# Two tiles of the first product at a time, by seven products of quarters in place of eight

## The chip, the cores and the metric

The kernel runs on one core of a Trainium2 chip. The metric is the device time of one execution in microseconds (us), shown as the median of several runs. Engines are named as in the profile: PE (TensorE) multiplies matrices, DVE (VectorE), ACT (ScalarE) and POOL (GpSimd) do everything else on the data, SP (SyncE) issues the transfers (DMA). Each engine works through its instructions in the order in which they were written; a wait stops everything behind it on that engine, SP's queue of transfers included. [...]

## The reference

Windowed attention (8 batches, 8 heads, 576 tokens, 64 channels a head), and on its output a feed-forward block for 4608 tokens:

```
x = attention(q, k, v)                     # 4608 x 512; half the heads see 32 neighbours, half every 4th of 128
h = x @ w_in                               # first product, 512 -> 1024
e = exp(h - max(h)); sm = e / (sum(e) + 1e-9)
solu = h * sm
ln = (solu - mean) / sqrt(var + 1e-6) * g_ln
out = ln @ w_out                           # second product, 1024 -> 512
```

## The kernel before

The 4608 tokens are 36 tiles of 128; attention is done in 32 units (a batch's pair of heads each). Matmuls run on fp32r operands. Since one such number doesn't hold all of an fp32, every operand is split into a high and a low part, and each product is three matmuls: high by high, high by low, low by high. So the first product of a tile (`moe_h`, L335 to L347) is 4 (parts of the 512 inputs) x 2 (halves of the 1024 outputs) x 3 = 24 matmuls of 128x128 by 128x512, and the second (`moe_o`, L473) is 24 as well.

The work is written out by hand as lists of words. `OPENING` (L50) holds the loading and splitting of the weights, the first units and tiles. Then the loop over tiles i = 6 to 35 (L582) runs the list `STEP` (L77) once a step: a word's name is the operation, its suffix says on which tile or unit (i the present tile, j and k the one and two before; n and m units of attention that run ahead). What a step does, in words:

- `ha hb hc hd`: first product of tile i on PE into banks 2 and 3 (L141; the same two banks for every tile from 3 on).
- `peak e gate mid var`: maximum on DVE (L352), exp on ACT (L359), h times exp with its sum on DVE (L366), minus the mean on DVE (L382), square on ACT (L387), then six tiny instructions on POOL that end in `rstd` (L388 to L395). `gate` is the last to read h from the banks.
- `forth back`: the tile goes to DRAM and comes back in another order (L439, L446, on SP's queue); `trA trB` turn it in 32x32 blocks on DVE (L455), `thA thB` make the high part on ACT (L463), `tlA tlB` the low part on POOL (L468). `o` is the second product on PE (L477), `out` scales on ACT (L487) and stores.
- `S mask max sub exp sum inv norm turn V`: one unit's attention: scores on PE (L211), mask, maximum, sums and the turn on DVE, `sub` on POOL (L250), exp on ACT (L254), and `V` on PE (L289).
- `xh xl`: high part of attention's output on ACT (L314), low part on DVE (L328), into the rings `x_hi` and `x_lo`, which hold two batches.
- `q v`: loads of a later unit (L165, L173), four buffers each.

The last tile is turned by PE (`t`, L412) instead of by way of DRAM.

## Time and profile before

| | us |
|---|---|
| median of 3 runs | 516.84 (516.23 to 517.65) |
| the profiled execution | 515.99 |
| its span, first to last instruction | 514.2 |
| PE busy, share of the span | 482.4, 94% |
| DVE, ACT, POOL busy | 343.0, 235.2, 218.5 |
| a first or second product without attention between, 24 matmuls | 5.44 |

The span is less than the execution's time by what lies around it, 1.8 us. Busy shares are means over stages with different limits. In the profile's rows, "out<-in" names tiles, L the line of the kernel; a group's row gives its count, busy time in us, the mean of one in ns, and the idle time ahead of it with what ended that.

### The profile page before, as it was taken

The page shows a single profiled execution, that of the slowest core. Times are in us where ns is not written, and L with a number is a line of the kernel's source. Part 1 is how long each engine was busy: PE and PEld are TensorE (multiplying, and loading weights), DVE is VectorE, ACT ScalarE, POOL GpSimd, SP SyncE. Part 2 cuts the span into 40 slices and gives each one's busy share as a digit, 9 for nine tenths or more (in the row PEclk, how much of TensorE's full clock was granted, in tenths as well). Part 3 has the DMA queues.
Part 4 walks back from the last instruction along what each step waited for, and adds up shares of the span by engine and source line. Part 5 has one row for each costly group of instructions (what it writes and reads, how often), then busy time and mean ns, then how long its engine had stood idle before and what let it go on. Part 6 is the DMA issues. An engine that isn't in the chain of part 4 may idle for free.

```text
span 514.2 us, 16377 instructions
## 1 busy us (share of the span) xinstructions
PE 482.4 (94%) x7132; PEld 388.2 (75%) x7132; DVE 343.0 (67%) x539; ACT 235.2 (46%) x387; POOL 218.5 (42%) x342
## 2 busy tenths in 40 slices
PE   1359989999999999999999999999999999999997
PEld 1237767788788888888888888888877888888885
DVE  3999999766467765577677766576677776444540
ACT  3857888633344443344433344343434444333351
POOL 1634775634444443444434443444444334333360
PEclk9999999999999999999999999999999999999999
DMA  7969186636585664556655564646644333333331
GB/s 274 402 234 376 46 286 197 197 125 212 169 273 184 184 180 137 153 183 182 182 169 172 181 182 137 183 154 184 177 141 134 105 106 91 111 108 103 108 98 61
DMA packets 47304, 88.37 MB, mean 172 GB/s; under 512 B 5504, under 2 KB 23808, under 8 KB 47232
## 3 DMA queue, kind: packets, MB, share of 16 engines
q1 hardware_dynamic: 47232, 87.32, 53.2%
q8 instruction: 56, 0.92, 0.7%
q14 instruction: 16, 0.13, 0.1%
HBM read 59.51 MB, written 27.79 MB: 170 GB/s over the span
## 4 chain that ended last, share of the span: by engine, by line
PE 90%; DMA 4%; DVE 3%; SPq 1%; issue 0%; ACT 0%; ACTq 0%; DVEq 0%
PE banks L341 40%; PE banks L477 39%; PE banks L289 6%; PE banks L211 5%; DMA raw<-w_in 1%; DMA kt<-kT 1%; DMA qt<-qT 1%; DVE low L526 1%; DVE pt L273 0%; DVE mag L534 0%; DVE rs L258 0%; PE banks L203 0%; DVE sm L247 0%; DVE mx L237 0%; SPq L165 0%
## 5 line engine op out<-in xcount | busy, mean ns | idle before, releaser
L341 PE MATMUL banks<-w_i,x_hi 128*128 128x512 f32 x576 | 183.1, 399 | 0.5 <-DVE mu L366 0.4
L477 PE MATMUL banks<-w_o,th 128*128 128x512 f32 x576 | 181.0, 395 | 0.0
L341 PEld LDWEIGHTS banks<-w_i,x_hi 128*128 128x128 f32 x576 | 106.6, 190 | 24.6 <-DVE mu L366 1.0
L477 PEld LDWEIGHTS banks<-w_o,th 128*128 128x128 f32 x576 | 106.2, 188 | 22.1 <-DVE w_o L548 0.2
L341 PE MATMUL banks<-w_i,x_lo 128*128 128x512 f32 x288 | 113.0, 393 | 0.0
L477 PE MATMUL banks<-w_o,tl 128*128 128x512 f32 x288 | 112.2, 390 | 0.0
L468 POOL TENSOR_TENSOR tl<-t,th 128x512 fp32r<-128x512 f32 x70 | 89.7, 1299 | 41.1 <-ACT th L463 41.1
L352 DVE TENSOR_REDUCE nmax<-banks 128x1 f32<-128x1024 f32 x36 | 44.0, 1223 | 65.2 <-PE banks L341 65.2
L254 ACT ACTIVATE sm<-sm 128x640 f32<-128x640 f32 x32 | 23.5, 736 | 94.5 <-POOL sm L250 94.0
L359 ACT ACTIVATE e<-banks,nmax 128x1024 f32<-128x1024 f32 x36 | 40.2, 1117 | 51.4 <-DVE nmax L352 50.8
L341 PEld LDWEIGHTS banks<-w_i,x_lo 128*128 128x128 f32 x288 | 54.5, 189 | 11.7
L477 PEld LDWEIGHTS banks<-w_o,tl 128*128 128x128 f32 x288 | 54.1, 188 | 11.7
L387 ACT ACTIVATE e<-t 128x1024 f32<-128x1024 f32 x35 | 37.2, 1062 | 55.2 <-DVE t L382 55.2
L366 DVE CUSTOM_DVE_ANT_0 t<-banks,e 128x1024 f32<-128x1024 f32 x36 | 43.9, 1219 | 17.1 <-ACT e L359 17.0
L289 PEld LDWEIGHTS banks<-pt,vt 32*64 32x64 f32 x2816 | 34.8, 138 | 18.9 <-issue 11.3
L463 ACT CAST th<-t 128x512 fp32r<-128x512 f32 x70 | 41.7, 619 | 15.9 <-DVE t L455 8.6
L455 DVE STREAM_TRANSPOSE t<-raw 128x512 f32<-128x512 f32 x70 | 44.9, 677 | 3.8 <-issue 2.6
L225 DVE TENSOR_TENSOR sm<-banks,mask_sb 128x640 f32<-128x640 f32 x22 | 18.1, 824 | 44.0 <-PE banks L211 43.8
L250 POOL TENSOR_TENSOR sm<-sm,mx 128x640 f32<-128x640 f32 x27 | 34.5, 1276 | 29.7 <-DVE mx L237 26.7
L289 PE MATMUL banks<-pt,vt 32*64 32x64 f32 (+3 forms) x2816 | 38.1, 234 | 7.7 <-DVE pt L273 7.7
L392 POOL TENSOR_SCALAR sq<-sq 128x1 f32<-128x1 f32 x36 | 7.7, 215 | 86.1 <-ACT e L387 85.6
L388 POOL TENSOR_SCALAR se<-se 128x1 f32<-128x1 f32 x36 | 8.7, 243 | 77.3 <-ACT e L359 76.6
(62 smaller groups left out, 474.7 us busy)
## 6 DMA issues: line engine op xcount, KB each, us to landing
mid<-t SPq DMA_DIRECT2D x140, 128.0 KB, 2.3
raw<-mid SPq DMA_DIRECT2D x35, 512.0 KB, 3.5
vt<-vw SPq DMA_DIRECT2D x32, 384.0 KB, 4.0
kt<-kT SPq DMA_DIRECT2D x32, 312.0 KB, 4.2
qt<-qT SPq DMA_DIRECT2D x32, 296.0 KB, 4.6
out<-ob SPq DMA_DIRECT2D x36, 256.0 KB, 2.1
t<-w_in SPq DMA_DIRECT2D x5, 512.0 KB, 7.2
t<-w_out SPq DMA_DIRECT2D x4, 512.0 KB, 6.7
```

The lines of the kernel that those rows point to most:

```text
L211: nc.tensor.matmul(out=ps[WIN * c : WIN * c + WIN, h, WQ * i : WQ * i + WQ], lhsT=qt[D * h : D * h + D, q0 : q0 + WIN], rhs=kt[D * h : D * ...
L250: eng.tensor_tensor(out=st[n]["sm"], in0=st[n]["sm"], in1=wide(mx), op=ALU.subtract)
L289: nc.tensor.matmul(out=ps_x[D * h : D * h + D, c, c0 : c0 + k1 - k0], lhsT=vt[WIN * c : WIN * c + WIN, i, D * h : D * h + D], rhs=pt[WIN * ...
L341: nc.tensor.matmul(out=ps_h(i)[:, half], lhsT=a[:, kt, xs], rhs=w_i[:, kt, half, part, :], start=(kt == 0 and k == 0), stop=(kt == KT - 1 ...
L352: nc.vector.tensor_reduce(out=nmax, in_=h, axis=AX.X, op=ALU.max, negate=True)
L359: nc.scalar.activation(out=e, in_=h, func=AF.Exp, bias=nmax, scale=1.0, accum_out=se)
L366: nc.vector.tensor_tensor_reduce(out=t, in0=h, in1=ms[i]["e"], scale=1.0, scalar=0.0, op0=ALU.mult, op1=ALU.add, accum_out=mu,)
L387: nc.scalar.activation(out=e, in_=t, func=AF.Square, accum_out=sq)
L455: nc.vector.transpose(out=turned(i)[:, cut(c)].rearrange("p k (a r) -> p k a r", r=WIN), in_=ms[i]["mv"].rearrange("p (a k s) -> p k a s", ...
L463: nc.scalar.copy(out=ms[i]["th"][:, cut(c)], in_=turned(i)[:, cut(c)])
L468: nc.gpsimd.tensor_tensor(out=ms[i]["tl"][:, cut(c)], in0=turned(i)[:, cut(c)], in1=ms[i]["th"][:, cut(c)].bitcast(F32), op=ALU.subtract,)
L477: nc.tensor.matmul(out=ps_o(i), lhsT=a[:, f, :], rhs=w_o[:, f, part, :], start=(f == 0 and k == 0), stop=(f == FT - 1 and k == 2),)
```

## The change

Tiles 0 to 13 are done as before. Tiles 14 to 35 go in eleven pairs (pair r is tiles 2r and 2r + 1, r from 7 to 17). For a pair, x is cut into four quarters (tile a or b, first or second half of the 512 inputs) and `w_in` into four. Seven products of sums of quarters, P1 to P7, give the four quarters of h that took eight before. A product of quarters is 6 matmuls, so 42 a pair in place of 48. It needs:

- sums of quarters of `w_in` (`fa` to `fh`), made once, on POOL, then their high parts on ACT (`Th`) and low parts on DVE (`Tl`). They are written behind the words of steps 8 to 12 (`BEHIND`). They take the room of two of four buffers of q, k and v, so units from 12 on have two.
- sums of quarters of x for each pair (`z1` to `z4`, on POOL, from fp32 values), split into high (`hS12 hS34`, ACT) and low (`lS12 lS34`, POOL); the plain quarters are split too (`hA1 hA2` on ACT, `lA1 lA2` on DVE). For that, x of units 16 and later stays in fp32 and is copied into the rings by a transfer (`xd`) from where ACT put it (`xf`). The sums for pair 7 stand ahead of step 13's words, their splits behind.
- sums of products: P1, P6, P7 and P4 follow one another in bank 0, P2 is in bank 1, P5 and P3 are in bank 2. ACT copies three stages out (`s1`, `s2`, `s5`), and DVE adds a bank to such a copy and takes the maximum in one instruction (`c11 c12 c22 c21`). So h stands in SBUF, and `e` and `gate` read it there.

The pairs have a list of their own, `PAIR`, and the last pair `LAST_PAIR`; the last tile goes by way of DRAM as the others do. Attention runs up to four units ahead throughout, and ends with unit 31 in pair 14; before, it ended with tile 30.

The diff, cut to its core (`a` and `b` are the pair's tiles, `c` and `d` those of the pair before, s the next pair; u, w, x and y units):

```diff
+AHEAD = {13: "z1.s z2.s z3.s z4.s "}
+BEHIND = {
+    8: "fa0 fb0 fc0 fd0", 9: "fe0 ff0 fg0 fh0 Th0 Th4 Th2 Th6", 10: "Tl0 Tl4 Tl2 Tl6 fa1 fb1 fc1",
+    11: "fd1 fe1 ff1 fg1 fh1 Th1 Th5 Th3 Th7", 12: "Tl1 Tl5 Tl3 Tl7",
+    13: "back.i hS12.s lS12.s hS34.s lS34.s",
+}
+PAIR = (
+    "P1.r trB.c P5.r S.u mask.u P2.r s1.r trA.c s5.r max.u c11.r q.u P6.r thB.c tlB.c V.x thA.c "
+    "trA.d tlA.c s2.r sub.u xf.x xd.x v.x exp.u P7.r P3.r trB.d z1.s sum.u S.w c12.r inv.u "
+    "thA.d pk.a thB.d oA.c tlA.d e.a mask.w tlB.d c22.r z2.s hS12.s gate.a oB.c mid.a max.w "
+    "forth.a P4.r norm.u z4.s z3.s c21.r hA1.s out.c sub.w var.a oA.d oB.d exp.w turn.u pk.b "
+    "V.y hA2.s e.b lA1.s sum.w hS34.s back.a inv.w lS12.s out.d gate.b mid.b norm.w lS34.s "
+    "forth.b q.w var.b back.b turn.w xf.y xd.y lA2.s v.y "
+)
+LAST_PAIR = (
+    "trA.c P1.r P2.r trB.c thA.c s1.r P6.r thB.c tlA.c tlB.c c11.r trA.d P5.r s2.r thA.d trB.d "
+    "P7.r s5.r thB.d tlA.d tlB.d P3.r c22.r P4.r c12.r pk.a c21.r e.a oA.c oB.c pk.b gate.a "
...
+POOL_WORDS = "z1 z2 z3 z4 lS12 lS34".split()
...
+    def t_value(j, kt, half):
+        add(nc.gpsimd, value(j), f32(w_i[:, kt, half, 0]), f32(w_i[:, kt, half, 1]))
+    def t_minus(j, a, b):
+        subtract(nc.gpsimd, value(j), value(a), value(b))
+    def t_hi(n):
+        nc.scalar.copy(out=t_high(n), in_=value(n // 2 + 1))
+    def t_lo(n):
+        subtract(nc.vector, t_low(n), value(n // 2 + 1), f32(t_high(n)))
...
+            if j == 1:
+                add(eng, out, x_of(b, 0, 2, c), x_of(b, 2, 4, c))
+            elif j == 2:
+                subtract(eng, out, v[1][:, :, c], x_of(a, 0, 2, c))
+            elif j == 3:
+                subtract(eng, out, x_of(a, 0, 2, c), x_of(b, 0, 2, c))
+            else:
+                subtract(eng, out, x_of(a, 2, 4, c), v[2][:, :, c])
...
+        bank = {1: 0, 6: 0, 7: 0, 4: 0, 2: 1, 5: 2, 3: 2}[j]
+        for kt in range(2):
+            for k, (pa, pb) in enumerate(((0, 0), (0, 1), (1, 0))):
+                nc.tensor.matmul(
+                    out=banks[:, bank],
+                    lhsT=left(pa, kt),
+                    rhs=right(pb, kt),
+                    start=j in (1, 2, 5) and kt == 0 and k == 0,
+                    stop=kt == 1 and k == 2,
...
+    def snap(i, half, bank):
+        nc.scalar.copy(out=part_h(i, half), in_=banks[:, bank])
+    def finish(i, half, bank, key):
+        mx = ms[i][key] = small.tile([P, 1], F32, name=key)
...
+        nc.vector.tensor_tensor_reduce(
+            out=out, in0=banks[:, bank], in1=zero.broadcast_to([P, 512]) if plain else out,
+            scale=1.0, scalar=LOWEST, op0=ALU.add, op1=ALU.max, accum_out=mx,
+        )
```

Where the change puts POOL's additions. Before, POOL's row between steps 9 and 10: the end of one step's `var`, then the low part `tl` of the tile whose second product comes next, then `sub`, then `var` again.

```order
L392 TENSOR_SCALAR sq_2504<-sq_2504 128x1
L393 TENSOR_TENSOR s2_2507<-s2_2507,sq_2504 128x1
L395 TENSOR_TENSOR rstd_2512<-s2_2507,mhalf_84 128x1
L468 TENSOR_TENSOR tl0_2551<-t0_2297,th0_2547 128x512 x2
L250 TENSOR_TENSOR sm0_2610<-sm0_2610,mx_2612 128x640
```

The same place on POOL now (`kt3`, `vt3` and `x` are buffers that hold the sums of quarters):

```order
L434 TENSOR_SCALAR sq_2501<-sq_2501 128x1
L435 TENSOR_TENSOR s2_2504<-s2_2504,sq_2501 128x1
L437 TENSOR_TENSOR rstd_2509<-s2_2504,mhalf_84 128x1
L512 TENSOR_TENSOR kt3_2339<-vt3_2344,kt3_2339 128x512
L512 TENSOR_TENSOR vt3_2344<-vt3_2344,qt3_2341 128x512
L515 TENSOR_TENSOR x_2543<-w_i_86 128x512
L512 TENSOR_TENSOR x_2543<-x_2543,vt3_2344 128x512
L482 TENSOR_TENSOR tl0_2561<-t0_2287,th0_2557 128x512 x2
L278 TENSOR_TENSOR sm0_2620<-sm0_2620,mx_2622 128x640
```

Four additions have come between `var` and `tl`. On ACT at the same place now stand four splits of these sums (L558) ahead of `th` (L477) and of the unit's exp (L282); the last, from `x`, needs the last of the four additions.

```order
L502 ACTIVATE ob_2538<-banks_90,rstd_2148 128x512
L558 CAST tp_2546<-qt3_2341 128x512
L558 CAST qt2_2548<-kt3_2339 128x512
L558 CAST more_2550<-vt3_2344 128x512
L558 CAST vt2_2552<-x_2543 128x512
L477 CAST th0_2557<-t0_2287 128x512 x2
L282 ACTIVATE sm0_2620<-sm0_2620 128x640
```

On ACT in the last pair, the copies of banks (L700: `s1`, `s2` into `t2`, `s5` into `t3`) stand between the high parts of the two tiles before (`th0` of tile 32, `th1` of tile 33):

```order
L477 CAST th0_6798<-t0_6614 128x512
L700 COPY t2_6800<-banks_90 128x512
L477 CAST th0_6798<-t0_6614 128x512
L700 COPY t2_6800<-banks_90 128x512
L477 CAST th1_6822<-t1_6617 128x512
L700 COPY t3_6831<-banks_90 128x512
L477 CAST th1_6822<-t1_6617 128x512
```

The third copy is behind the first half of tile 33's high part; before, the only word of the last tile at such a place was its exp.

## The prediction

> **What bounds the kernel now.** I read the page first: its span and its line of busy shares.

> ```profile
> span 514.2 us, 16377 instructions
> PE 482.4 (94%) x7132; PEld 388.2 (75%) x7132; DVE 343.0 (67%) x539; ACT 235.2 (46%) x387; POOL 218.5 (42%) x342
> ```

> PE alone is near the span. So I read the chain of waits in order of time over one step of the loop, that of tile 10 (below, 0 of a step is the first matmul of its first product):

> ```profile
> 169.44 2.72 PE banks L341 x12
> 172.16 0.97 PE banks L211 x64
> 173.13 2.95 PE banks L341 x12
> 176.08 1.13 PE banks L289 x76
> 177.21 5.71 PE banks L477 x24
> 182.91 1.13 PE banks L341 x5
> ```

> The chain never leaves PE: first product in two halves with the scores between them, attention, second product; 182.91 - 169.44 = 13.47 us a step, and 2.72 / 12 = 0.227 us a matmul. Fewer matmuls pay as long as the other engines keep up. How much room they have I read from their timeline in the same step:

> ```profile
> 171.12 2.53 POOL L468 TENSOR_TENSOR tl<-t,th 128x512 fp32r<-128x512 f32 x2 [1.14 <-ACT th L463]
> 174.93 1.26 POOL L250 TENSOR_TENSOR sm<-sm,mx 128x640 f32<-128x640 f32 x1 [1.28 <-DVE mx L237]
> 176.22 0.74 ACT L254 ACTIVATE sm<-sm 128x640 f32<-128x640 f32 x1 [4.58 <-POOL sm L250]
> 177.43 1.12 ACT L359 ACTIVATE e<-banks,nmax 128x1024 f32<-128x1024 f32 x1 [0.48 <-DVE nmax L352]
> 178.45 0.19 ACT L359 ACTIVATION_READ_ACCUMULATOR e<-banks,nmax 128x1 f32 x1
> 179.93 0.08 DVE L366 DVE_READ_ACCUMULATOR2_ANT mu<- 128x1 f32 x1
> 180.24 0.75 DVE L382 TENSOR_SCALAR t<-t,mu 128x1024 f32<-128x1024 f32 x1
> 182.05 0.18 ACT L387 ACTIVATION_READ_ACCUMULATOR e<-t 128x1 f32 x1
> 182.42 0.85 DVE L273 STREAM_TRANSPOSE pt<-sm 128x640 f32<-128x640 f32 x1
> 182.88 0.57 POOL L395 TENSOR_TENSOR rstd<-s,mhalf 128x1 f32<-128x1 f32 x1
> ```

> Each of these engines works in written order, so this is a loop that closes through POOL. Back to back it takes: tl 2.53, sub 1.26, to the end of exp 0.77 (176.19 to 176.96), e right behind exp on ACT 1.21 (177.43 to 178.64), to the end of gate 1.37 (180.01): 7.14 us. Then mid 0.98 (180.99), var 1.24 (182.23), POOL's end of var 1.22 (183.45): 3.44. Together 10.58, so a step of 13.47 leaves 2.89 us. PE waits on the loop at two places: the second product needs tl, and the next step's first product needs gate, since all these tiles use banks 2 and 3.

> **The change, part by part.** *Matmuls.* Eleven pairs do 7 x 6 = 42 matmuls in place of 48: 66 x 0.227 = 15.0 us less. The last tile's transposes on PE go too, in the chain

> ```profile
> 498.68 0.87 PE banks L412 x8
> ```

> 0.9; together 15.9 us less.

> *The sums of weights, steps 8 to 13.* 16 additions of 128x512 on POOL, eight splits each on ACT and DVE, then ten additions of 128x256 for the first pair. They stand behind POOL's var and ahead of the next step's tl and sub, inside the loop. The nearest row for an addition is half of the tl row, 1.26 us; for a split on ACT it is a th, and for a tiny addition POOL's square, among the groups by form; for a split on DVE it is L534 in the opening:

> ```profile
> L463 ACT CAST th<-t 128x512 fp32r<-128x512 f32 x70 | 41.7, 619 | 15.9 <-DVE t L455 8.6 <-PE banks L477 7.3
> L390 POOL TENSOR_TENSOR s<-se 128x1 f32<-128x1 f32 x36 | 7.5, 209 | 3.0
> ```

> ```profile
> 6.88 0.69 DVE L534 SCALAR_TENSOR_TENSOR mag<-mag,low 128x512 int32<-128x512 int32 x1
> ...
> 19.44 1.51 DVE L534 SCALAR_TENSOR_TENSOR mag<-mag,low 128x512 int32<-128x512 int32 x1
> ```

> POOL is free 0.54 us into a step (183.45 - 182.91), DVE behind gate 3.26 us later (183.27, end of turn). Step by step, each time from that step's start:
> Step 9: four additions, 0.54 + 5.04 = 5.58; gate ends 7.14 later, 12.72, before 13.47: nothing lost, but POOL is free only at 16.16, 2.69 into step 10.
> Step 10: four additions, 7.73. ACT has four splits ahead of th, and the last needs the last addition: 8.35, th 8.97, gate 16.11. Lost 2.6.
> Step 11: POOL is free at 3.44, but its first addition overwrites what DVE's second split reads: 3.26 + 2 x 0.69 = 4.64. Three additions, 8.42; gate 15.56. Lost 2.1.
> Step 12: 3.44 + five additions = 9.74; split and th 1.24, gate 18.12. Lost 4.7.
> Step 13: ten small additions, each between 0.21 and 1.26 us; I take the middle, 0.73, since half the elements are summed. They start behind the first split on DVE, 3.95; 11.25; gate 18.39, POOL free at 21.83, lS12 23.09. P5 of pair 7 needs lS12 for its third matmul and so ends at 24.0, unhindered at 13.47 + 2.72 = 16.2. Lost 7.8.
> Sum 17.2 us. Bounds: 14 if the small additions take 0.5, 24 if they take 1.26 and DVE and POOL hinder each other twice. That they do is in the two rows of L534: 0.69 alone, 1.51 when POOL had begun this just before:

> ```profile
> 19.15 1.26 POOL L250 TENSOR_TENSOR sm<-sm,mx 128x640 f32<-128x640 f32 x1 [0.41 <-ACT sm L241]
> ```

> *Pairs 7 to 13, with attention.* PE needs two steps less 1.36, 25.6 us. DVE loses two peaks and two x_lo and gains four additions of 128x512 from PSUM with a maximum, two splits (1.1 by the 0.69 row) and two tiny instructions (0.3):

> ```profile
> L352 DVE TENSOR_REDUCE nmax<-banks 128x1 f32<-128x1024 f32 x36 | 44.0, 1223 | 65.2 <-PE banks L341 65.2
> L366 DVE CUSTOM_DVE_ANT_0 t<-banks,e 128x1024 f32<-128x1024 f32 x36 | 43.9, 1219 | 17.1 <-ACT e L359 17.0
> L328 DVE TENSOR_TENSOR x_lo<-banks,x_hi 128x576 fp32r<-128x576 f32 x29 | 21.7, 748 | 7.1 <-ACT x_hi L314 7.1
> ```

> By windows, core 0 from 250 to 300 us (PE, PEld, DVE, ACT, POOL):

> ```profile
> 250.00:300.00 50.00, 50.00 (x850) 40.45 (x850) 35.83 (x57) 19.99 (x32) 19.67 (x33) 1.00 0.56 173
> ```

> Such an addition lies between half of L366, 0.6, and all of it, 1.2; I take 0.77, near the half: 3.1 for four. 1.1 + 0.3 + 3.1 - 2.45 - 1.5 = +0.55. DVE was busy 35.83 of 50, 19.3 in two steps; now some 19.9 of 25.6, about 22.5 with three collisions of 0.8. It fits, and PE loses nothing here (0 to 7 us over seven pairs). POOL's four sums, their splits and the three snapshots on ACT have the two second products (11.4) to hide behind. x of units 16 and later goes by a copy on SP's queue, of qt's size,

> ```profile
> qt<-qT SPq DMA_DIRECT2D x32, 296.0 KB, 4.6
> ```

> and its sums are needed a pair's half later. Uncovered, it would cost up to 4.6 a pair.

> *Pairs 15 and 16, without attention.* P7 follows P6 directly on bank 0 and must wait until ACT has copied it (s2). The nearest case is the last output:

> ```profile
> 510.09 0.39 PE L477 MATMUL banks<-w_o,tl 128*128 128x512 f32 x1
> 510.66 0.69 ACT L487 ACTIVATE ob<-banks,rstd 128x512 f32<-128x512 f32 x1 [4.84 <-PE banks L477]
> ```

> 510.48 to 511.35 is 0.87, some 0.9 with the way back: 1.8 for two (1.2 to 2.4).

> *The last pair.* Tile 33 goes to DRAM behind output 31 on SP's queue (forth.b stands behind out.d). A tile's way there and back, and the turn that waits for it:

> ```profile
> 487.30 1.78 SPq L439 DMA_DIRECT2D mid<-t  x4
> 489.12 0.45 SPq L488 DMA_DIRECT2D out<-ob  x1
> ```

> ```profile
> 494.87 1.31 DVE L455 STREAM_TRANSPOSE t<-raw 128x512 f32<-128x512 f32 x2 [0.37 <-DMA raw<-mid]
> ```

> 7.57 us. Output 31 ends 0.87 into pair 17 and issues for 0.45, so tile 33 is back at 8.9. ACT's order is th of tile 33, then P5's snapshot s5: 8.9 + 0.65 + 0.62 + 0.7 = 10.9, and P3 needs s5. Ahead of it P1, P2, P6, P5 and P7 end at 7.5 (6.8 and 0.7 lost on s1, which stands behind tile 32's th): P3 loses 3.4. Then tile 34 goes c12 0.8, maximum 0.15, e 1.3, gate 1.37, mid 0.98 behind P3, 3.3 behind P4; with 7.57 + 0.65 + 0.62 + 1.26 its tl is there 13.4 behind P4, where PE has second products for 10.9: lost 2.1, its first two matmuls counted. Sum 6.2 (3 to 9).

> Sum: -15.9 + 17.2 + 1.8 + 6.2 = +9.3. The profiled execution took 515.99 us, its span and 1.8 around it: 525.3. It lies 0.85 below the median of 516.84; against that, 526.1.

> [...]

> **The rivals.** *The sums find room (not slower, 0.20).* Place: POOL between var and tl. They hide wholly where a step's additions take up to 2.89 us, 0.7 each. For it: POOL is busy only 42%, and step 9 absorbs four. Against: 1.26 a row, and they stand ahead of tl. If 7 of the 17.2 stay, and 3 of the last pair's 6.2: -15.9 + 7 + 1.8 + 3 = -4.1, 512.7; if 2 stay, 508. *DVE becomes the bound (slower still, 0.15).* [...] *PE slows behind its waits (0.10).* The chain of the opening has

> ```profile
> 40.65 4.95 PE banks L341 x12
> ```

> 0.41 us a matmul in place of 0.227, behind thin work. Three waits with twelve such each: 3 x 2.2, 532.7. That the matmuls don't go is excluded: the order has them gone.

> **How the numbers follow.** My case has 0.55: 526.1, and 521 to 535 by its bounds. The first rival has 0.20: 0.17 faster and 0.03 within 0.3% (1.5 us, about what a measurement here can tell from none). With the two slower ones, 0.25, slower is 0.80. The range reaches from 513, the first rival's milder end, to 536, the upper bounds with a slow PE.

> **What would show it.** Right: in steps 10 to 13 L512 and L515 on POOL right ahead of tl (L482), PE idle before the second product (L491) for tl and before the first (L385) for gate; 7 us lost by the end of P5 of pair 7; in pair 17 P3 waiting for s5. Wrong: PE unbroken from 156 us into the first pair, or DVE without idle time in pairs 7 to 13.

## The result, and the profile after

The changed kernel takes 558.61 us in the median (four runs, 552.94 to 559.46), beside 516.55 (516.23 to 517.65) for the kernel before in the same session: ratio 1.079, 95% interval 1.071 to 1.086. The forecast was 526.1, with a range of 513 to 536: the sign is right, the size is far off. The profiled execution is the fastest of the four, 552.94, so 37.0 us are to be explained in its span. In the times below, a run more than 1.5% above the fastest of its kernel counts as slow and stays out of the median. First the page, its span, its busy shares and the clock granted to PE in 40 slices:

```profile
span 551.2 us, 16611 instructions
...
PE 488.4 (89%) x7058; PEld 384.0 (70%) x7058; DVE 380.1 (69%) x640; ACT 275.0 (50%) x470; POOL 350.1 (64%) x443
...
PEclk9999999999999987989999999899999999999799
```

PE has fewer matmuls and more busy time, and in five slices a lower clock; before, all were 9. DVE and POOL stay far from full, so PE waits for an order of things, not for an engine's total work. For whom, PE's waits by line say (before, its timeline has none above 0.1 us past 81 us):

```profile
PE banks L491 <- ACT ob L502: 9.6, 5, 2.6
...
PE banks L239 <- ACT x L353: 5.5, 7, 1.2
PE banks L491 <- ACT th L477: 5.2, 3, 2.7
PE banks L682 <- ACT t L700: 4.8, 4, 3.3
PE banks L491 <- POOL tl L482: 4.8, 3, 3.5
```

The total in us, times, the longest. Waits for `th` and `tl` (third and fifth row) are for the most part those that the sums of weights were to bring; the copies of outputs and of x (first and second) were not in the forecast. By stages, from PE's timeline, each against the unhindered pace of the forecast (13.47 a step with attention, 10.88 without, 1.36 less a pair):

| stretch | took | unhindered | lost | forecast |
|---|---|---|---|---|
| tile 8's first matmul to the end of P5 of pair 7 | 103.2 | 83.5 | 19.7 | 17.2 |
| the rest of pair 7, pairs 8 to 13 | 191.9 | 176.3 | 15.5 | 0 (0 to 7) |
| pair 14 | 24.3 | 21.5 | 2.8 | 0 |
| pairs 15 and 16 | 44.1 | 40.8 | 3.3 | 1.8 |
| last pair, to the last matmul | 42.4 | 31.3 | 11.1 | 6.2 (3 to 9) |

The 31.3 are 138 matmuls at 0.227. The losses add up to 52.4. Less the 15.9 for matmuls and transposes, and 0.8 for the opening and the end, that is 35.7 of the 37.0. The rest lies mostly in the pace: steps whose `V` has 80 matmuls in place of 96 need 13.31 unhindered, not 13.47, so the first two stretches lost a little more than the table has.

**Steps 8 to 13.** The chain of waits in step 10, in order of time:

```profile
171.13 1.26 POOL kt L512
172.39 0.07 issue
172.46 1.29 POOL vt L512
173.76 1.25 POOL x L515
...
175.09 1.28 POOL x L512
...
176.39 0.62 ACT vt L558
177.01 0.53 ACT th L477
...
177.60 2.52 POOL tl L482 x2
180.12 1.23 POOL sm L278
```

Four additions and the last split stand between POOL's var and tl, as foreseen. Steps 10 to 12 and step 13 with P5 lose 2.9, 3.3, 5.7 and 7.8 us, where 2.6, 2.1, 4.7 and 7.8 were forecast.

**Pair 8**, from the timeline of all engines (start, duration, engine; in brackets the idle time ahead of it and what ended it):

```profile
272.97 1.20 SPq L347 DMA_DIRECT2D x_hi<-x  x1
...
278.40 0.64 ACT L353 COPY x<-banks 128x576 f32<-128x576 f32 x1 [3.40 <-DMA x_hi<-x]
...
279.06 0.47 SPq L347 DMA_DIRECT2D x_hi<-x  x1
...
283.49 1.18 POOL L515 TENSOR_TENSOR qt<-x_hi 128x256 f32<-128x256 f32 x1 [7.06 <-DMA x_hi<-x]
...
284.63 3.57 POOL L482 TENSOR_TENSOR tl<-t,th 128x512 fp32r<-128x512 f32 x2
...
288.16 0.72 POOL L512 TENSOR_TENSOR qt<-qt,x_hi 128x256 f32<-128x256 f32 x1
...
288.91 0.62 ACT L640 CAST w_i<-qt 128x512 fp32r<-128x512 f32 x1 [6.10 <-POOL qt L512]
...
289.44 0.61 ACT L654 CAST x_lo<-x_hi 128x512 fp32r<-128x512 f32 x1
...
289.96 0.68 ACT L502 ACTIVATE ob<-banks,rstd 128x512 f32<-128x512 f32 x1
...
290.69 0.50 PE L491 MATMUL banks<-w_o,th 128*128 128x512 f32 x1 [2.64 <-ACT ob L502]
```

It is one long line over SP, ACT, POOL and PE. There is one buffer for x on its way to the rings. Its first copy goes out at 272.97, and ACT can fill it again only when that has landed, at 278.40. The second copy holds `z1` on POOL until 283.49, and behind `z1` in POOL's order stand both tl of tile 15 and `z2`; behind `z2`, ACT's `hS12`, `hA1` and then the copy of output 14 out of bank 3, which the next second product needs. Pairs 8, 10 and 12 take 30.5, 30.7 and 29.0 us, pairs 9, 11 and 13 take 26.7, 26.6 and 26.0: in the even ones the unit that arrives in the pair is the last of a batch, and the next sums need it at once.

**The last pair.** The snapshot s5 (L700) on ACT and P3 on PE, from the same view:

```profile
514.45 0.62 ACT L477 CAST th<-t 128x512 fp32r<-128x512 f32 x1 [4.26 <-DVE t L469]
514.97 0.58 ACT L700 COPY t<-banks 128x512 f32<-128x512 f32 x1
...
515.60 2.93 PE L682 MATMUL banks<-w_i 128*128 128x512 f32 x6 [3.30 <-ACT t L700]
...
518.33 0.63 PE L682 MATMUL banks<-vt,vt 128*128 128x512 f32 x1
...
518.76 0.63 PE L682 MATMUL banks<-low,vt 128*128 128x512 f32 x1
```

P3 starts 10.8 us into the pair with 3.3 idle ahead of it (10.9 and 3.4 in the forecast). But then a matmul comes every 0.43 us in place of 0.227, and what the wait cost nearly doubles.

### The profile page after: what moved, and what is told of

The parts are those of the page before. It is cut to its first block, busy times and chain, and to the rows that moved or that the text cites. A ratio compares the mean times of both kernels' runs of the same rounds, so it can differ in the third digit from the quotient of the medians.

```text
span 551.2 us, 16611 instructions
## 1 busy us (share of the span) xinstructions
PE 488.4 (89%) x7058; PEld 384.0 (70%) x7058; DVE 380.1 (69%) x640; ACT 275.0 (50%) x470; POOL 350.1 (64%) x443
## 4 chain that ended last, share of the span: by engine, by line
PE 31%; DMA 20%; POOL 19%; DVE 13%; issue 7%; ACT 6%; SPq 4%; DVEq 0%; ACTq 0%; POOLq 0%
PE banks L491 19%; POOL tl L482 7%; PE banks L385 7%; DMA x_hi<-x 5%; DMA mid<-t 5%; DVE t L412 3%; SPq L453 3%; PE banks L682 2%; DMA raw<-mid 2%; POOL qt L512 2%; POOL qt L515 2%; POOL sm L278 2%; DMA x_lo<-x 2%; DVE t L424 2%; PE banks L239 2%
## 5 line engine op out<-in xcount | busy, mean ns | idle before, releaser
L491 PE MATMUL banks<-w_o,th 128*128 128x512 f32 x576 | 188.3, 409 | 15.5 <-ACT ob L502 9.6
L491 PEld LDWEIGHTS banks<-w_o,th 128*128 128x128 f32 x576 | 111.5, 197 | 43.0 <-ACT ob L502 12.3
L482 POOL TENSOR_TENSOR tl<-t,th 128x512 fp32r<-128x512 f32 x72 | 96.5, 1355 | 55.6 <-ACT th L477 55.6
L491 PE MATMUL banks<-w_o,tl 128*128 128x512 f32 x288 | 116.8, 406 | 4.9 <-POOL tl L482 4.8
L385 PE MATMUL banks<-w_i,x_hi 128*128 128x512 f32 x224 | 73.2, 409 | 1.3 <-DVE mu L412 1.2
L491 PEld LDWEIGHTS banks<-w_o,tl 128*128 128x128 f32 x288 | 56.4, 196 | 19.5 <-POOL tl L482 7.2
L477 ACT CAST th<-t 128x512 fp32r<-128x512 f32 x72 | 42.8, 618 | 46.3 <-DVE t L469 38.9
L286 DVE TENSOR_REDUCE rs<-sm 128x10 f32<-128x640 f32 x32 | 26.1, 816 | 39.2 <-ACT sm L282 39.2
L385 PEld LDWEIGHTS banks<-w_i,x_hi 128*128 128x128 f32 x224 | 41.6, 193 | 11.4 <-DVE mu L412 2.2
L317 PEld LDWEIGHTS banks<-pt,vt 32*64 32x64 f32 x2816 | 35.7, 138 | 18.8 <-issue 7.6
L239 PEld LDWEIGHTS banks<-kt,qt 64*32 64x32 f32 x2560 | 30.1, 112 | 21.5 <-issue 10.5
L385 PE MATMUL banks<-w_i,x_lo 128*128 128x512 f32 x112 | 44.7, 399 | 0.0
L282 ACT ACTIVATE sm<-sm 128x640 f32<-128x640 f32 x32 | 23.6, 737 | 42.1 <-POOL sm L278 41.6
L239 PE MATMUL banks<-kt,qt 64*32 64x64 f32 x2560 | 36.1, 238 | 8.9 <-ACT x L353 5.5
L502 ACT ACTIVATE ob<-banks,rstd 128x512 f32<-128x512 f32 x36 | 24.7, 685 | 36.5 <-PE banks L491 29.8
L412 DVE CUSTOM_DVE_ANT_0 t<-t,e 128x1024 f32<-128x1024 f32 x22 | 34.1, 1552 | 10.0 <-ACT e L403 9.9
L424 DVE TENSOR_SCALAR t<-t,mu 128x1024 f32<-128x1024 f32 x31 | 35.0, 1128 | 1.1
L682 PE MATMUL banks<-w_i,x_lo 128*128 128x512 f32 x116 | 31.9, 402 | 0.0
## 6 DMA issues: line engine op xcount, KB each, us to landing
qt<-qT SPq DMA_DIRECT2D x32, 296.0 KB, 5.5
```

Source lines behind the costliest of these rows:

```text
L239: nc.tensor.matmul(out=ps[WIN * c : WIN * c + WIN, h, WQ * i : WQ * i + WQ], lhsT=qt[D * h : D * h + D, q0 : q0 + WIN], rhs=kt[D * h : D * ...
L317: nc.tensor.matmul(out=ps_x[D * h : D * h + D, c, c0 : c0 + k1 - k0], lhsT=vt[WIN * c : WIN * c + WIN, i, D * h : D * h + D], rhs=pt[WIN * ...
L385: nc.tensor.matmul(out=ps_h(i)[:, half], lhsT=a[:, kt, xs], rhs=w_i[:, kt, half, part, :], start=(kt == 0 and k == 0), stop=(kt == KT - 1 ...
L412: nc.vector.tensor_tensor_reduce(out=t, in0=h, in1=ms[i]["e"], scale=1.0, scalar=0.0, op0=ALU.mult, op1=ALU.add, accum_out=mu,)
L424: nc.vector.tensor_scalar(out=dst, in0=src, scalar1=mu, scalar2=None, op0=ALU.subtract)
L477: nc.scalar.copy(out=ms[i]["th"][:, cut(c)], in_=turned(i)[:, cut(c)])
```

## The experiments

Their times stand against its 558.6, and the kernel before ran beside each. The first seven are edits of the changed kernel.

**The places of the weight work in steps 8 to 13.**

```diff
-AHEAD = {13: "z1.s z2.s z3.s z4.s "}
-BEHIND = {
-    8: "fa0 fb0 fc0 fd0", 9: "fe0 ff0 fg0 fh0 Th0 Th4 Th2 Th6", 10: "Tl0 Tl4 Tl2 Tl6 fa1 fb1 fc1",
...
+WITHIN = {
+    8: {"sub": "fa0 fb0 fc0", "V": "fd0"}, 9: {"sub": "fe0 ff0 fg0 fh0"},
+    10: {"tlB": "Th0 Th4 Th2 Th6", "sub": "Tl0 Tl4 Tl2 Tl6 fa1 fb1 fc1 fd1"},
...
```

The word ahead of the colon is the one of `STEP` behind which they stand.

> Same instructions as the changed kernel; only the places of the weight work in steps 8 to 13 differ: POOL's additions stand behind sub in their step, ACT's splits behind th, DVE's behind the maximum. My theory (the place in the loop costs it): from tile 8's first product to the end of P5 of pair 7 the changed kernel takes 103.2 us (141.35 to 244.59) where 5 steps of 13.47 and 16.2 would be 83.5, so 19.7 lost; here at most 4 of them stay, and the time falls by 16 to 20, to 539 to 543. Rival (the amount of work on POOL, and what it takes DVE and POOL from each other, wherever it stands): half or more stays, 548 or above.

Measured 543.4 (541.1 to 547.5), 15.2 less, just outside the range expected. POOL in step 11 of this kernel, and PE at P5 of pair 7:

```profile
188.38 2.55 POOL L483 TENSOR_TENSOR tl<-t,th 128x512 fp32r<-128x512 f32 x2 [1.15 <-ACT th L478]
190.89 1.26 POOL L279 TENSOR_TENSOR sm<-sm,mx 128x640 f32<-128x640 f32 x1
192.11 1.30 POOL L513 TENSOR_TENSOR kt<-vt,kt 128x512 f32<-128x512 f32 x1
193.49 1.30 POOL L513 TENSOR_TENSOR vt<-vt,qt 128x512 f32<-128x512 f32 x1
```

```profile
229.42 0.73 PE L683 MATMUL banks<-tp,w_i 128*128 128x512 f32 x2 [2.51 <-POOL w_i L513]
```

The stretch of the table's first row falls from 103.2 to 88.1 us. The same additions cost a step 0.6 at the most behind sub, where POOL would wait for var; 4.6 of the 19.7 stay, 2.5 of them the wait for the low part of S1 and S2. That the place in the loop is the cause is shown.

**Three ways to cut the line of pair 8.** First POOL's order (z1 and z2 behind tl of the second tile):

```diff
-P7.r P3.r trB.d z1.s sum.u S.w
+P7.r P3.r trB.d sum.u S.w
...
-mask.w tlB.d c22.r z2.s hS12.s
+mask.w tlB.d c22.r z1.s z2.s hS12.s
```

> Only z1 and z2 of the next pair move on POOL from ahead of the second half-tile's tl to behind it, in pairs 7 to 16; the copies stay. If the order on POOL turns the late copy into a wait of PE, the wait ahead of the second tile's second product (2.6, 2.2, 2.0 in pairs 8, 10, 12) goes and 1 us at the scores stays: 6 to 9 us less, 549 to 553. If the copies cost by being in the way (queue, memory) and not by that order, less than 3 us changes.

Measured 549.3 (548.6 to 550.0), 9.3 less. The waits for output copies fall from 9.6 to 5.0 us, those for x rise from 5.5 to 7.6. Then the copy of x itself, sooner on SP's queue:

```diff
-    "forth.b q.w var.b back.b turn.w xf.y xd.y lA2.s v.y "
+    "forth.b q.w var.b turn.w xf.y xd.y back.b lA2.s v.y "
```

> Only the order on SP's queue changes: the copy of a pair's second x goes out ahead of the load of tile b's turned values, which waits there for its own store to land. In pair 8 of the changed kernel that x lay ready at 270.34 and its copy was issued at 272.97. If the copy's lateness is what the even pairs lose, each of pairs 8, 10, 12 gains 1 to 2.5 us: 552 to 556. If the load of the turned values, now 0.5 to 1.2 us later, is as much needed: no change.

Measured 554.2 (553.7 to 556.8), 4.4 less, but these runs overlap with those of the changed kernel (552.9 to 559.5). The waits for x nearly go (1.1 us), those for output copies stay (8.7). Then the bank:

```diff
-        return banks[:, LAST_BANKS.get(i, i % 2 if i < PAIRED - 2 else 3)]
+        return banks[:, LAST_BANKS.get(i, i % 2 if i < PAIRED - 2 else (3, 1)[i % 2])]
```

> Only the PSUM bank of the second product of odd tiles changes from 13 on: bank 1 in place of bank 3, so that it needs no copy of the even tile's output ahead of it. The waits for that copy in the changed kernel are 2.64, 2.20, 1.98 in pairs 8, 10 and 12 and 2.22, 0.1, 0.6 in pairs 14 to 16, with some 2 us at a slow pace behind them. If it is the bank that couples PE to ACT's late copies: 7 to 11 us less, 548 to 552. If the same lateness reaches PE another way (tl of the second tile, the scores): under 4 us less.

Measured 548.5 (547.2 to 551.6; a fourth run took 555.6), 10.1 less. PE's waits for copies of outputs are gone from its list, and its first row is now

```profile
PE banks L239 <- ACT x L353: 8.5, 8, 2.1
```

So each cut takes away the wait at which it was aimed, and part of what it frees is lost at the next late instruction.

**ACT's order.** var of the pair's odd tile, whose square waits for DVE's mid, moves from ahead of x to the next pair:

```diff
-    "forth.b q.w var.b back.b turn.w xf.y xd.y lA2.s v.y "
+    "xf.y xd.y forth.b q.w turn.w back.b lA2.s v.y "
...
-s1.r trA.c s5.r max.u
+s1.r trA.c s5.r var.d max.u
```

> The changed kernel with one edit, on ACT: var of a pair's odd tile moves into the next pair, so that the copy of x of the second unit doesn't stand behind its square, which waits for DVE's mid; that x then goes out on SP ahead of the store of tile b. In pair 8 of the changed kernel that x was copied at 269.7, behind a square that began at 268.66, though its attention product had ended at 267.1; the pair's first x then found the buffer free only at 278.4. If this order couples DVE's late mid to PE, the waits at the scores for x (5.5 in all) fall below 2 and z1 of pairs 8, 10 and 12 comes 2 us earlier: 4 to 8 us less, 550 to 555. If it is only one of several late things in the same place, under 3 us: 556 or more.

Measured 555.5 (555.3 to 559.4), 3.2 less: between the two cases, less than I had expected of this coupling, and again not clear of the changed kernel's own runs. No wait for x is left at the scores, but the first row of PE's waits is

```profile
PE banks L491 <- ACT ob L502: 13.4, 5, 4.4
```

in place of 9.6. This one, by itself, mostly moved the wait.

What the pairs themselves took in the profiled executions says more than the medians. The last column but one is the clock granted to PE over pairs 7 to 13.

| kernel | pairs 7 to 13 | granted clock | of it pairs 8, 10 and 12 |
|---|---|---|---|
| the changed kernel | 195.9 | 0.99 | 90.2 |
| other places in steps 8 to 13, the same words in these pairs | 204.0 | 0.97 | 94.7 |
| matmuls in the gaps (below), the same words in these pairs | 203.4 | 0.96 | 94.6 |
| another last pair (below), the same words in these pairs | 203.0 | 0.97 | 93.3 |
| z1 and z2 behind tl | 193.5 | 0.99 | 82.8 |
| x sooner on SP | 201.1 | 0.97 | 94.5 |
| the other bank | 191.7 | 0.99 | 79.9 |
| var in the next pair | 197.9 | 0.97 | 93.8 |

The same words take 195.9 to 204.0, with the lower clock in the longer ones. Only POOL's order and the bank lie below that, and only they shorten pairs 8, 10 and 12. That the copy's place on SP or ACT's order alone gains anything is not shown.

**Matmuls in the gaps.** They write a bank whose content is not read any more.

```diff
+FILL = {(11, "V.m"): 6, (12, "o.k"): 11, (13, "o.k"): 15}
...
-P7.r s5.r thB.d tlA.d tlB.d P3.r
+P7.r s5.r thB.d tlA.d tlB.d F14 P3.r
```

> Matmuls whose result nobody reads are put where PE waits: 6 ahead of the attention product of step 11, 11 and 15 ahead of the second products of steps 12 and 13, 14 ahead of P3 of the last pair. In the changed kernel what follows those waits is slow: second products of 7.24, 8.63 and 7.91 us in place of 5.74, P3 with P7's end 5.49 in place of 3.0. Theory (PE is slow after it waited, whatever it works on): with the gaps filled these take 5.8, 5.8, 5.8 and 3.1; the steps' time changes by under 2 us, as POOL's loop sets it there, and the last pair is 3 us shorter. Rival (the operands come slowly, through collisions in SBUF): the durations stay, and the time grows by what is put in.

Measured 576.9 in its one run, and 15 of that come from where the matmuls of step 13 read: a place of x_hi that unit 16's copy fills, for which they stood waiting. The other places tell what was asked. The second product of step 12 in the changed kernel and in this one (L694 are the matmuls put in):

```profile
211.88 1.22 PE L491 MATMUL banks<-w_o,th 128*128 128x512 f32 x2 [2.68 <-ACT th L477]
...
213.82 1.05 PE L491 MATMUL banks<-w_o,th 128*128 128x512 f32 x2
214.67 0.63 PE L491 MATMUL banks<-w_o,tl 128*128 128x512 f32 x1
```

```profile
209.01 2.79 PE L694 MATMUL banks<-w_i,x_hi 128*128 128x512 f32 x11
212.33 0.73 PE L492 MATMUL banks<-w_o,th 128*128 128x512 f32 x2 [0.52 <-ACT th L478]
...
214.02 0.63 PE L492 MATMUL banks<-w_o,th 128*128 128x512 f32 x2
214.48 0.39 PE L492 MATMUL banks<-w_o,tl 128*128 128x512 f32 x1
```

Three matmuls take 1.28 us after the wait and 0.69 with the gap filled; the product 8.6 us there, and here 5.3 for all but its first two. P3 of the last pair:

```profile
538.26 3.33 PE L694 MATMUL banks<-w_i,x_hi 128*128 128x512 f32 x14
541.65 1.66 PE L683 MATMUL banks<-w_i 128*128 128x512 f32 x6
```

1.66 in place of 2.93. The granted clock was 0.50 from 211.3 to 217.9 us in the changed kernel, and 1.00 in the same stretch of this one. So PE was slow there because it had waited, not for its operands. That filling the gap shortens the last pair is not shown: it takes 40.0 here and 42.4 in the changed kernel, but 39.6 to 40.3 in the traces of the first four edits, which have the same list. In step 12 little came of it: from tile 9's first matmul to tile 13's it is 64.2 us in place of 65.7, since POOL's loop sets that time.

**The list of the last pair.**

```diff
-    "trA.c P1.r P2.r trB.c thA.c s1.r P6.r thB.c tlA.c tlB.c c11.r trA.d P5.r s2.r thA.d trB.d "
-    "P7.r s5.r thB.d tlA.d tlB.d P3.r c22.r P4.r c12.r pk.a c21.r e.a oA.c oB.c pk.b gate.a "
+    "trA.c P1.r P2.r trB.c thA.c s1.r P5.r thB.c tlA.c tlB.c c11.r P6.r s5.r s2.r P3.r c12.r "
+    "pk.a e.a P7.r c22.r oA.c P4.r gate.a mid.a forth.a back.a trA.d thA.d trB.d thB.d var.a "
...
```

> Only the list of the last pair changes: P5 ahead of P6, P3 ahead of P7, s5 ahead of tile 33's th on ACT, P4 behind half of tile 32's second product, tile 33's turn behind tile 34's gate. In the changed kernel this pair takes 42.4 us from P1 to the last matmul (504.84 to 547.23), 3.3 of it idle for s5, 1.8 for th and tl of tile 34, about 5 at a slow pace behind these. Theory: 33 to 35 us here, 7 to 9 less in all, 549 to 552, with P3 at 1.4 us for its six matmuls. Rival (tile 33 comes back too late whatever the order, and tile 34's chain sets the end): 3 us or less.

One run took 543.5, the other three 553.3 to 558.2, so the times settle nothing by themselves; PE's timeline of the profiled one (558.2) does. The pair takes 35.6 us (516.91 to 552.47), 6.8 less than in the changed kernel and 4.1 to 4.8 less than in the first four edits, with P1 to P7 unbroken. What is left are waits for tl of the last three tiles, 1.5, 0.7 and 0.6.

**All together, and what was then in sight.** The next kernel takes these remedies (without ACT's order), with three more moves:

```diff
-exp.u P7.r P3.r trB.d
+exp.u P3.r P7.r trB.d
...
-inv.w lS12.s out.d gate.b
+inv.w lS12.s gate.b
...
-forth.b q.w
+forth.b out.d q.w
...
+            words = words.replace("P5.r S.u mask.u P2.r", "S.u mask.u P2.r P5.r")
```

The last line is for the first pair.

> All remedies together: the weight work placed inside the steps, z1 and z2 behind tl, copies of x and stores of tile b ahead on SP, P3 ahead of P7, P5 behind P2 in the first pair, the second bank, the other list for the last pair. If the losses are those of the theory (19.7 in the steps, 16.7 in the pairs with attention, 5 without, 10 in the last) and each remedy takes the most of its own: 515 to 524. If one engine's work is the bound in the pairs (DVE or POOL busy over 90%), it stays above 530.

Measured 529.6 (526.4 to 531.8), ratio 1.024 (1.020 to 1.029): between the two cases. Its trace still showed ACT's order (6.6 us for x, 3.5 for snapshots behind var), so the next one adds that (this diff and those behind it are against the kernel just before):

```diff
-    "forth.b out.d q.w var.b turn.w xf.y xd.y back.b lA2.s v.y "
+    "out.d xf.y xd.y forth.b q.w turn.w back.b lA2.s v.y "
...
-    13: {"tlB": "z1.s", "sub": "z2.s z3.s z4.s", "e": "hS12.s hS34.s lS12.s", "out": "back.i lS34.s"},
+    13: {"tlB": "z1.s", "sub": "z2.s z3.s", "e": "hS12.s z4.s lS12.s", "out": "hS34.s back.i lS34.s"},
```

> The kernel with all remedies, and what its own trace still showed: var of a pair's odd tile moves into the next pair (its square on ACT held x of the second unit and the snapshot s1 for up to 4 us, as it waits for DVE's mid), the copy of x goes out ahead of the store of tile b, and in step 13 and pair 7 the low parts of S1 and S2 stand ahead of other sums on POOL. Waits of PE that should go: 2.4 and 0.6 in pair 7, 2.2 and 1.1 in pair 8, 2.0 in pair 10, 1.6 and 2.0 in pairs 16 and 17, with 5 us at a slow pace behind them. If ACT's order is their cause: 513 to 519, beside 529.6. If these waits only move to the next late instruction: 524 or more.

Measured 519.7 (ten runs), ratio 1.005 (1.003 to 1.008): just above the first case. From P1 to the next pair's P1, pair 9 takes 25.6 us (281.93 to 307.55) and pair 10 25.4 (to 332.98), where two steps took 26.94: the matmuls saved are there in full once nothing is late. Two more kernels only change order again (in the last pair P5 ahead of P2 and tl ahead of var; in pairs 7 and 8 whatever was still waited for).

```diff
-            words = words.replace("P5.r S.u mask.u P2.r", "S.u mask.u P2.r P5.r")
+            words = words.replace("V.y hA2.s", "V.y xf.y hA2.s").replace("out.d xf.y", "out.d")
...
-    "trA.c P1.r P2.r trB.c thA.c s1.r P5.r thB.c tlA.c tlB.c c11.r P6.r s5.r s2.r var.d P3.r c12.r "
+    "P1.r P5.r P2.r s1.r s5.r trA.c trB.c thA.c thB.c tlA.c tlB.c c11.r P6.r s2.r var.d P3.r "
...
```

> The kernel before this with the waits that its own trace still shows taken away by order alone: the low parts of S1 and S2 on POOL ahead of z3 (then P5 of the first pair may stand where the change had it, and P2 finds its bank copied: 1.45 us there), x of pair 7's second unit on ACT ahead of the next tile's exp (1.82 at the scores of pair 8, and 2 at a slow pace behind), in the last pair P5 ahead of P2 and both snapshots ahead of tile 32's th (0.97 and 1.79), and tile 33's tl on POOL ahead of tile 34's var, which waits for ACT's square (1.49, and part of 0.74). Together 8 to 11 us of 519.7 if these are causes: 508 to 512, faster than the kernel before the change (517). If the waits move on to other instructions: 515 or more.

```diff
+MOVES = (
+    (7, 7, ("s5.r var.d", "s5.r hS34.r lS34.r")),
...
+    (13, 15, ("out.c sub.w var.a", "out.c sub.w lS12.s var.a")),
...
```

> By order alone again, against the waits of PE in the trace of the kernel before this (1.22 for s1 in pair 7; 1.20, 0.45 and 0.95 in pair 8 with 1.6 at a slow pace; 0.6 and 0.4 for the low parts of S1 and S2 in pairs 15 to 17; 0.65 for s2 in 16 and 17): s1 and s5 ahead of the high part of S3 and S4 in pair 7; in pair 7 output 13 ahead of the next exp on ACT and the turn of the scores ahead of gate; the low parts of S1 and S2 ahead of var on POOL in pairs 13 to 15; s2 ahead of th in 15 to 17. Together 6 to 8 us of 515.6 if the waits are their own causes: 507 to 510. If they only move on: 514 or more.

The first took 515.6 us (12 runs; ratio 0.998, 0.996 to 1.0005), the second 516.1 beside 517.6 (0.998, 0.996 to 0.9999): 0.2% ahead of the kernel before at best, no more than can be told from none. Both came out as their second case had it: the waits moved on. The page of the first:

```profile
span 513.1 us, 16637 instructions
...
PE 474.3 (92%) x7058; PEld 375.3 (73%) x7058; DVE 380.4 (74%) x640; ACT 274.7 (54%) x470; POOL 352.5 (69%) x443
```

PE is 14 us less busy than in the changed kernel, on the same 7058 matmuls. In the second, the longest wait of PE behind the opening is in pair 8, 3.4 us for the scores' way through DVE, behind a turned tile that came late from DRAM.

The direct test of x's copies is open. A kernel in which ACT writes x into the rings without them gave no time; the forecast for it was 546 to 549 if the copies are what pairs 8, 10 and 12 lose, and 555 or above if the pairs simply hold too much work. A second buffer for x was not tried, and no run shows whether there is room for one.

## Why the prediction was wrong

- *66 matmuls, 15.0 us.* Right: 25.4 us for a pair with nothing late.
- *Sums of weights, 17.2 (14 to 24).* Right, in mechanism, place and size: 19.7, and moving them alone brought 15.2 back.
- *Pairs 7 to 13, 0 (0 to 7).* **Here it failed**: 15.5, and 22 to 23 in the three other traces with the same words. The step was "its sums are needed a pair's half later" for the copies of x, and "POOL's four sums, their splits and the three snapshots on ACT have the two second products (11.4) to hide behind". I had set the work of each engine against the time of a pair, and it does fit: DVE, the fullest, is busy 148 of the 192 us. But the sums stand in one line with what PE needs: z1 ahead of tl on POOL, hS12 and hA1 ahead of the output's copy on ACT, x behind a square that waits for DVE. In every second pair the copy is needed at once. Of PE's idle time there, 6.8 us are waits for copies of outputs and 5.5 waits for copies of x; a term of nothing stood for both. The cuts at POOL's order and at the bank took 9.3 and 10.1 us out, clear of the spread of the runs, so these two links are shown; the queue and ACT's order (4.4 and 3.2) are not clear of it, and rest on the trace of pair 8. How much of the 15.5 each link holds alone stays open, as they cover one another.
- *Pairs 15 and 16, 1.8.* P7's wait for s2 shows as 0.68 of idle time a pair, where 0.9 was forecast. Of the rest of the 3.3, 0.7 are waits for the same copy of an output; of pair 14's 2.8 it is 2.2.
- *Last pair, 6.2 (3 to 9).* The waits are nearly as worked out: 0.2 for s1, 3.3 for P3 (at 10.8 us) and 1.8 for tile 34, where 0.7, 3.4 and 2.1 were forecast. The 4.9 above the 6.2 are mostly the pace behind them: P3 and P4 took 2.6 us more than at full pace, the second products of tiles 32 and 34 0.5 and 1.6 more. That was the rival with 0.10, priced there at 2.2 a wait; it holds, and beside the other losses, not in their place. In the traces of the first four edits the same list loses 8.3 to 9.0.
- *From the profiled execution to the median.* The 5.7 us between 552.9 and 558.6 were not in the forecast. The 7 to 8 us by which the same words took longer in other traces, at a lower clock, would cover them; no slower execution of this very kernel has a trace.
- *The rival in which DVE becomes the bound* is out: in pairs 7 to 13 DVE was busy 148 of the 192 us, and at its fastest gate takes the same with both sources in SBUF (`t` and `e`) as with one in PSUM, where the banks are, 1164 and 1161 ns (the rows are below), though beside POOL's work it took 1.55 us in the mean. So is the one in which the sums find room.

## What to carry to other kernels

Work that fits an engine's time can still cost all of it: ask of each instruction put in which one stands behind it on its engine, and whether PE waits for that. Put it where its engine would wait anyway, and give the step that ends a chain (a store, a var, a statistic) a place behind what feeds PE. In the last pair a wait of PE of 3.3 us was followed by 2.6 us lost to the slow pace of P3 and P4, and a wait of 2.64 us in pair 8 by none; so a change that trades matmuls for waits has to be counted with and without such a loss behind each. Here 15 us of matmuls paid for some 1 us in the end, which is hardly to be told from none.

## What the runs showed of the hardware

**Pace after a wait.** In the changed kernel a matmul takes 0.43 us in place of 0.227 for 3 to 6 us behind waits of 1.1 to 3.5 us; but behind the wait of 2.64 us in pair 8 the pace was full, and behind one of 2.20 (at 346.41) it was full for 1.3 us, then half for some 3. The granted clock (the last figure but two in a row of the view by windows) goes with it, behind the wait at 211.88 and behind the one in pair 8:

```profile
211.30:217.90 6.60, 5.89 (x13) 0.50 0.07 26
290.60:297.00 6.40, 6.31 (x87) 1.00 0.36 124
```

Among the kernels with many waits, the runs of the changed one lie 6.5 us apart, those of the one with the other last pair 14.7, and those of the one with z1 and z2 behind tl 1.4; the kernel before had 1.4 in four runs and 5.2 in seventeen of a later session. In the one with the other last pair, pairs 7 to 13 took 7.1 us longer than in the changed kernel on the same words, at a granted clock of 0.97 in place of 0.99. Over the whole span its run of 543.5 us had a clock of 0.987, and its three longer ones (553.3 to 558.2) 0.969 to 0.974; but in the changed kernel the run of 552.9 and that of 558.0 both had 0.972, and the two of 559.2 and 559.5 had 0.960 and 0.966. So most of the longer runs, not all, have the lower clock; how much the pace takes, and how much the waits that follow it, is not shown.

**DVE and POOL together.** gate, all its executions with both sources in SBUF (`t`, `e`) and with one in PSUM (`banks`; duration minimum/median/maximum in ns):

```profile
L412 DVE CUSTOM_DVE_ANT_0 t<-t,e x22: 1164/1346/2346, 255.6 to 526.8; 128x1024 f32<-128x1024 f32 x22
L412 DVE CUSTOM_DVE_ANT_0 t<-banks,e x14: 1161/1224/1225, 56.4 to 237.2; 128x1024 f32<-128x1024 f32 x14
```

At its fastest it takes the same from SBUF as from PSUM, 1164 and 1161 ns. But it and an addition on POOL get in each other's way: begun under one, gate took 2.22 us, and an addition begun under gate took 2.22 in place of 1.29. First the end of pair 7, then that of pair 8 (the timeline of all engines):

```profile
265.71 1.16 DVE L412 CUSTOM_DVE_ANT_0 t<-t,e 128x1024 f32<-128x1024 f32 x1
265.79 2.22 POOL L512 TENSOR_TENSOR w_i<-qt,w_i 128x512 fp32r<-128x512 f32 x1
...
294.13 1.29 POOL L512 TENSOR_TENSOR w_i<-qt,w_i 128x512 fp32r<-128x512 f32 x1
...
294.29 2.22 DVE L412 CUSTOM_DVE_ANT_0 t<-t,e 128x1024 f32<-128x1024 f32 x1 [0.16 <-ACT e L403]
...
295.39 2.27 POOL L512 TENSOR_TENSOR w_i<-kt,w_i 128x512 fp32r<-128x512 f32 x1
```

In these rows the one that began first kept its own time, and the one that began under it took longer by about what was left of the first: gate first, 1.16 and then 2.22 for the addition; an addition first, 1.29 and then 2.22 for gate, and 2.27 for the next addition, which began under gate. With one source in PSUM gate never took over 1.23, beside POOL's tl too: 1.22 at 131.23, in the middle of a pair of tl that took 2.55 from 130.75.
